# Two transformer layers on one core: which row maxima stand beside the projections, as sums of two key tiles, and in what order attention issues the rest

## The chip, the cores and the metric

The kernel runs on one core of a Trainium2 chip. The metric is the device time of one execution in microseconds (us). TensorE (PE) does the matrix products, VectorE (DVE) and ScalarE (ACT) read their results out of PSUM, GpSimd (POOL) works on SBUF alone, SyncE (SP) issues nearly all transfers. PSUM has eight banks; one bank holds one 128x512 result in fp32.

## The reference

Two rounds of attention and a squared-ReLU MLP, each behind a layer norm, with the same weights in both rounds:

```python
B, S, D, H = 1, 2048, 640, 32          # head width 20; F = 1536 in the MLP
qkv = layernorm(x) @ wqkv
scores = einsum("bhqd,bhkd->bhqk", q, k) * Dh ** -0.5
p = softmax(scores, axis=-1)
x = x + einsum("bhqk,bhkd->bhqd", p, v).reshape(B, S, D) @ wo
x = x + square(relu(layernorm(x) @ w1 + b1)) @ w2 + b2
```

## The kernel before

The kernel does the two layers one after the other. Each has three stages: projections (`qkv`), attention, and the output projection with the MLP. Most operands are split into a high and a low fp32r part, so that a projection is fifteen matmuls (five slices of D, three products each).

**Heads and blocks.** Four heads make a group `g` (8 of them), 512 queries a block of queries `qb` (4 of them). A block `t = 4 g + qb` is the unit of attention: 32 blocks, each with 16 key tiles of 128. Softmax needs the largest score of each query first. The scores for that are computed by queries: one matmul for 128 queries (`sub`, 4 of them), one head and 512 keys (`c`, 4 of them). Heads lie in two halves of the PE array (`par` 0 and 1), so that two matmuls run side by side, and a *pair* is both of them, for one `(p, sub)`. One block and one `c` are 8 pairs.

**Plain maxima and doubles.** A plain maximum is one matmul and one DVE reduction over 512 keys (line 679 beside the projections, `smax_two`; line 665 in attention, `smax`). A double takes two key tiles at once. `kd` holds the difference of key tiles 2i+1 and 2i; PE multiplies it with q (line 654), ACT takes the ReLU (`step_two`, line 687), PE multiplies tile 2i, and DVE adds both and takes the maximum (`both_two`, line 694). Since a + relu(b - a) = max(a, b), one DVE instruction, followed by a read of its accumulator on the same line, does the work of two reductions. "d" stands for tiles 0 and 1, "e" for 2 and 3. The differences are made on POOL when the projection of the second tile is read out of PSUM (`proj_end`, line 398 and the next two), stored to `d_kd` in DRAM and loaded again by heads (`load_kd`).

**The projection stage.** `UNITS` lists 40 units (10 slices of the outputs by 4 blocks of 512 tokens), the first four slices (`FIRST`) for each block of tokens first; sixteen steps for V follow. From unit 4 on each matmul is done as two halves of 64 rows that run side by side, the second half 22 steps behind the first (`Halves.LAG`). After each matmul `between(cost)` is called; when the sum of costs (1 for a unit's matmul, 0.65 for one of V) has used up the pace, `some()` puts one step of maxima into PE's queue: a plain pair (pace 4.2) or one half of a double, `step_two` or `both_two` (pace 1.97 each). `STEPS[n]` says after which unit which tiles are loaded and which lists of maxima begin. Before, 32 plain pairs begin after units 4, 5, 9 and 11, and 22 lists of doubles (176 pairs) after unit 12. Nothing waits in software: PE, DVE, ACT and SP each run their own queue in order.

**Attention.** The order of operations in attention is a string, `ORDER_OF_BLOCK`, repeated until the stage is done: `a` and `b` are one score matmul by keys of either half with its exponential on ACT (128x512), `S` is both with one exponential of 128x1024, `m` and `n` are one plain maximum of either half for a later block, and `V` is the product of weights and values for one key tile (eight matmuls, line 763, in column tiles of 32). I call the stretch from one `V` to the next a period; each has four scores on average. The banks are chosen by `Clock`, a small model of the queues in the kernel itself. `todo` lists the maxima that the projection stage has not done.

Of the kernel before, what the change touches and what calls it, by code (L numbers as in the profile page):

```python
# [9 lines left out]
F32R = mybir.dt.float32r  # L10
# [29 lines left out]
def tile_layers(  # L40
# [185 lines left out]
            sp.put(raw, k * 4, k * 4 + 2, 2, eng_hi, eng_lo)  # L226

    d_qk = dram.tile([2, 2, D, S], F32R, name="d_qk")
    d_kd = dram.tile([2, 2, 2 * P, QB], F32R, name="d_kd")
    d_v = dram.tile([S, H, 32], F32, name="d_v")  # L230
    d_o = dram.tile([D, NQB, 2 * QB], F32R, name="d_o")
    d_one = dram.tile([2, 2, QB], F32R, name="d_one")
# [150 lines left out]
    def proj_end(pos, tb, dst):  # L383
        ev = slot([P, 2, QB], F32R, "ev")
        which, jj = divmod(ORDER[pos], 5)
        rows = slice(jj * P, (jj + 1) * P)
        kd = None
        if which and pos < FIRST:


            if tb % 2 == 0 and jj == 0:
                keys["of"] = slot([P, 2, QB], F32, "kf")
            kf = keys["of"][:, jj, :]
            r = xtile("r")[:, :QB] if tb % 2 else kf
            split_on_pool(ev[:, 0, :], ev[:, 1, :], dst, r, nc.scalar.copy)
            if tb % 2:
                kd = slot([P, 2, QB], F32R, "kd")
                nc.gpsimd.tensor_sub(kf, r, kf)
                pool_hi(kd[:, 0, :], kf)
                pool_lo(kd[:, 1, :], kf, kd[:, 0, :].bitcast(F32))  # L400
                if jj:
                    del keys["of"]
        else:
            if tb or pos >= FIRST:
                split_on_pool(
                    ev[:, 0, :], ev[:, 1, :], dst, None, nc.scalar.copy if pos < FIRST else None
                )
# [423 lines left out]
    def prep_job():  # L831
# [13 lines left out]


    DOUBLE = [
        [],
# [5 lines left out]
    ]  # L854
    PARTLY = {g * NQB + qb for x in DOUBLE for g, qb, c in x}

    FIRST = 4
    PLAIN_PACE = 4.2  # L860
    DOUBLE_PACE = 1.97
    STEPS = {
        2: [("tiles", (0, 0, 0))],
        4: [("plain", (0, 0, 0)), ("tiles", (1, 0, 0))],
        5: [("plain", (1, 0, 0))],
        7: [("tiles", (0, 0, 1))],
        9: [("plain", (0, 0, 1)), ("tiles", (1, 0, 1))],
        10: [("tiles", (0, 1, "d"))],
        11: [("plain", (1, 0, 1))],
        12: [("double", 1)],  # L870
        15: [("double", 2)],
        19: [("double", 3)],
    }
    UNITS = [(tb, pos) for tb in range(NQB) for pos in range(FIRST)]
    UNITS += [(tb, pos) for pos in range(FIRST, 10) for tb in range(NQB)]

    def qkv(first, x_src, rest):

        pending, groups, work = [], [], []
        double, twos, begun = [], [], []  # L880
        left.update((t, 4) for t in range(NBLK))
        done.clear()
# [50 lines left out]
        def end_group(x):  # L933
            g, qb, c = x
            t = g * NQB + qb
            rest = [w[0] for w in work[:1] + twos[:1]] + [w[0][0] for w in begun[:1]] + groups + double
            if t == 0:
                left[t] -= 1 if c in range(4) else 2
                if left[t] == 0:
                    mrows_max(t)  # L940
                    store = mrows(t)
                    later_rows.append((state["n"] + 60, store))
                    later_rows.append((state["n"] + 75, lambda: mrows_load(t)))
            if (t or left[t]) and all(y[:2] != (g, qb) for y in rest[:4]):
                del q_t[t]
            use = {(y[0], y[2]) for y in rest + coming}
            use |= {(h, 2 * "de".index(y)) for h, y in use if y not in range(4)}
            for y in [y for y in k_t if y[0] == g and y not in use]:
                if g < 2 or y[1] not in range(4):
                    del k_t[y]  # L950
# [10 lines left out]
                queue.extend((x, p, sub) for p, sub in PAIRS)  # L961
            return queue.pop(0)

        def one():
            w = following(groups, work)
            if w:
                (g, qb, c), p, sub = w
                smax_two(g * NQB + qb, p, sub, c)
                done.add((g * NQB + qb, p, sub, c))
                if (p, sub) == PAIRS[-1]:  # L970
                    end_group(w[0])

        def some():


            while later_rows and later_rows[0][0] <= state["n"]:
                later_rows.pop(0)[1]()
            if begun and (len(begun) > 1 or not (double or twos)):
                w, r = begun.pop(0)
                (g, qb, x), p, sub = w  # L980
                t = g * NQB + qb
                both_two(t, p, sub, x, r)
                c = 2 * "de".index(x)
                done.update([(t, p, sub, c), (t, p, sub, c + 1)])
                if (p, sub) == PAIRS[-1]:
                    end_group(w[0])
                return DOUBLE_PACE
            if groups or work:
                one()
                return PLAIN_PACE  # L990
# [17 lines left out]
        for n, (tb, pos) in enumerate(UNITS):  # L1008
# [11 lines left out]
            for what, x in STEPS.get(n, ()):  # L1020
                if what == "tiles":
                    tiles(x)
                elif what == "plain":
                    groups.append(x)
# [6 lines left out]
        for tt in range(NKT):  # L1031
# [15 lines left out]
            if tt == 11:  # L1047
                load_k(3, 0, True)
                load_q(3 * NQB)
            if tt == 12:  # L1050
                for c in range(1, 4):
                    load_k(3, c, True)
            if tt == 13:
                load_q(1)
                load_q(3 * NQB + 1)
        while run.behind:
            run.catch()
        while double or twos or begun:
# [11 lines left out]


    ORDER_OF_BLOCK = (
        "bbannaVbamnabmVnabmnabVSnanbmVnambabmVSbmnaVSnabmVSnSmVbmamnSVbmanbanVan"
        "abmbmVbambannVbmabanmVSmbanVSnabmVSnSmVm"
    )

    def attention(first, x_src, first_rows):
        last = NBLK * NKT
# [117 lines left out]
        for o in "abab":  # L1196
            op(o)
        while state["done"] < last:
            for o in ORDER_OF_BLOCK:
                op(o)  # L1200
        assert min(sm_n) == len(todo)
        q_t.clear()
# [227 lines left out]
```

## Time and profile before

| what | value |
|---|---|
| median of 3 runs | 3586.14 us (3582.98 to 3586.66) |
| profiled execution, its own time | 3588.35 us |
| span of its trace | 3586.5 us |
| mean granted clock of TensorE | 0.998 |
| busy: PE, DVE, ACT, POOL | 99%, 74%, 75%, 23% |
| projection stage, first and second layer | to 341.7 us; 1805.9 to 2122.3 us |
| attention, first and second layer | 341.7 to 1386.0 us; 2122.3 to 3168.2 us |

The span runs from the first to the last instruction; 1.85 us of the profiled execution lie outside it. The ends of the stages are the first and the last exponential (line 758) and the first matmul of the second layer's projections. A busy PE is not PE at its peak, since ends of matmuls are modelled: what PE does is read from the distance between starts.

### The profile page before, as it was taken

How to read it: one execution, taken by the hardware profiler on the slowest of the kernel's cores; microseconds unless marked ns; L12 is line 12 of the kernel's file. 1: busy time of each engine (PE TensorE's matmuls, PEld its weight loads, DVE VectorE, ACT ScalarE, POOL GpSimd, SP SyncE). 2: the span in 40 equal slices, each digit the busy share in tenths (PEclk: the TensorE clock that was granted, in tenths of full speed). 3: DMA queues.
4: the chain of work that ended last, by engine and by line, in shares of the span. 5: the costliest groups of instructions: out<-in, count | busy, mean ns of one | idle time of the engine just before them, and what ended most of it. 6: DMA issues, size and time to landing. Idle time of an engine off the chain costs nothing.

```text
span 3586.5 us, 71057 instructions
## 1 busy us (share of the span) xinstructions
PE 3557.8 (99%) x25544; PEld 2151.0 (60%) x25544; DVE 2650.9 (74%) x5208; ACT 2694.0 (75%) x4742; POOL 836.0 (23%) x945
## 2 busy tenths in 40 slices
PE   8999999999999999999999999999999999999999
PEld 7998333333333336889989973333333333378998
DVE  8998888888888871445569988888888888625443
ACT  3888999999999994122238889999999999932221
POOL 5440334312121210122143201212112212101110
PEclk9999999999999999999999999999999999999999
DMA  7766454422212136622367552222222121365220
GB/s 242 231 223 198 138 170 147 141 78 71 60 49 60 54 102 218 234 74 74 103 193 226 191 174 67 79 73 63 67 83 56 42 60 51 111 234 209 75 81 37
DMA packets 282800, 433.85 MB, mean 121 GB/s; under 512 B 71188, under 2 KB 130324, under 8 KB 282448
## 3 DMA queue, kind: packets, MB, share of 16 engines
q1 hardware_dynamic: 281920, 427.61, 38.3%
q8 instruction: 202, 3.31, 0.4%
q10 hardware_dynamic: 528, 1.70, 0.2%
q14 instruction: 150, 1.23, 0.1%
HBM read 284.48 MB, written 144.68 MB: 120 GB/s over the span
## 4 chain that ended last, share of the span: by engine, by line
PE 94%; DMA 2%; DVE 1%; ACT 1%; SPq 0%; issue 0%; POOL 0%; ACTq 0%; DVEq 0%; POOLq 0%
PE banks L763 27%; PE banks L336 22%; PE banks L748 18%; PE banks L654 17%; PE banks L365 5%; PE banks L356 4%; ACT e L758 0%; SPq L76 0%; DMA k<-d_qk 0%; PE banks L461 0%; DMA ot<-d_o 0%; DVE r L1278 0%; DVE h L257 0%; ACT r L1277 0%; DVE mx L679 0%
## 5 line engine op out<-in xcount | busy, mean ns | idle before, releaser
L758 ACT ACTIVATE e<-banks 128x512 f32<-128x512 f32 (+1 forms) x3460 | 2040.8, 687 | 49.4 <-PE banks L748 11.5
L665 DVE TENSOR_REDUCE mx<-banks 128x1 f32<-128x512 f32 x2560 | 1620.7, 685 | 326.1 <-PE banks L654 294.4
L763 PE MATMUL banks<-e,vg 128*32 128x512 f32 x8192 | 1097.3, 605 | 6.1 <-ACT e L758 5.4
L654 PE MATMUL banks<-k,q 60*128 60x512 f32 x3392 | 1080.6, 411 | 6.3 <-DMA q<-d_qk 1.8
L748 PE MATMUL banks<-q,k 62*128 62x512 f32 x4096 | 1045.5, 441 | 0.0
L748 PEld LDWEIGHTS banks<-q,k 62*128 62x128 f32 x4096 | 514.5, 185 | 741.8 <-ACT e L758 467.6
L654 PEld LDWEIGHTS banks<-k,q 60*128 60x128 f32 x3392 | 579.3, 185 | 208.0 <-ACT e L758 64.7
L694 DVE CUSTOM_DVE_ANT_0 rl<-banks,rl 128x512 f32<-128x512 f32 x704 | 456.7, 688 | 24.5 <-PE banks L654 6.2
L687 ACT ACTIVATE rl<-banks 128x512 f32<-128x512 f32 x704 | 381.0, 601 | 52.3 <-PE banks L654 41.8
L763 PEld LDWEIGHTS banks<-e,vg 128*32 128x32 f32 x8192 | 163.8, 108 | 362.3 <-issue 262.6
L336 PE MATMUL banks<-w,h 128*128 128x320 f32 x2304 | 348.9, 310 | 2.6 <-DVE h L257 2.5
L1277 ACT ACTIVATE r<-banks,b_t 128x512 f32<-128x512 f32 x96 | 66.1, 688 | 377.8 <-PE banks L336 224.7
L336 PEld LDWEIGHTS banks<-w,h 128*128 128x128 f32 x2304 | 339.2, 188 | 11.4 <-DVE h L257 6.4
L336 PE MATMUL banks<-xnT,w 128*128 128x512 f32 x1440 | 329.7, 389 | 0.0
L365 PE MATMUL banks<-xnT,wqk 64*128 64x512 f32 x1080 | 327.3, 393 | 1.6 <-DVE turned_t L358 1.6
L356 PE MATMUL banks<-xnT,wqk 64*128 64x512 f32 x1080 | 327.2, 394 | 0.0
L336 PEld LDWEIGHTS banks<-xnT,w 128*128 128x128 f32 x1440 | 269.5, 188 | 55.3
L807 POOL TENSOR_TENSOR few<-few,minus_t 128x16 f32<-128x16 f32 x62 | 179.8, 2900 | 225.6 <-DMA few<-d_s 225.6
L654 PE MATMUL banks<-kd,q 60*128 60x512 f32 x704 | 208.9, 398 | 0.2
L365 PEld LDWEIGHTS banks<-xnT,wqk 64*128 64x128 f32 x1080 | 201.2, 187 | 12.9 <-DVE turned_t L358 2.1
L268 POOL CAST mr<-nt 128x32 fp32r<-128x32 f32 x64 | 13.4, 210 | 824.6 <-DVE nt L720 794.6
L356 PEld LDWEIGHTS banks<-xnT,wqk 64*128 64x128 f32 x1080 | 198.8, 186 | 10.2 <-issue 1.7
(91 smaller groups left out, 2789.5 us busy)
## 6 DMA issues: line engine op xcount, KB each, us to landing
q<-d_qk SPq DMA_DIRECT2D x888, 80.0 KB
d_qk<-ev SPq DMA_DIRECT2D x80, 512.0 KB
k<-d_qk SPq DMA_DIRECT2D x456, 80.0 KB
x<-d_x SPq DMA_DIRECT2D x96, 320.0 KB
d_o<-ot SPq DMA_DIRECT2D x248, 80.0 KB
ot<-d_o SPq DMA_DIRECT2D x38, 512.0 KB
d_v<-v SPq DMA_DIRECT2D x32, 512.0 KB
vg<-d_v SPq DMA_DIRECT2D x32, 512.0 KB
```

Source lines behind the costliest of these rows:

```text
L336: nc.tensor.matmul(dst, a, b, start=(n == 0), stop=(n == last))
L356: nc.tensor.matmul(dst, a[:64], b[:64], start=start, stop=last)
L365: nc.tensor.matmul(dst, a, b, start=False, stop=last, skip_group_check=True)
L654: nc.tensor.matmul(dst, q_t[t][b : b + 60, p, sub * P : (sub + 1) * P], k_t[t // NQB, c][b : b + 60, p, :], start=True, stop=True,)
L665: nc.vector.tensor_reduce(maxima(t)[:, 2 * p + par, sub, c : c + 1], dst, axis=AX.X, op=ALU.max)
L687: nc.scalar.activation(r, dst, AF.Relu)
L694: nc.vector.tensor_tensor_reduce(out=r[par], in0=dst, in1=r[par], scale=1.0, scalar=LEAST, op0=ALU.add, op1=ALU.max, accum_out=maxima(t)[: ...
L748: nc.tensor.matmul(dst, k_t[t // NQB, kt // 4][b : b + 62, p, (kt % 4) * P : (kt % 4 + 1) * P], q_t[t][b : b + 62, p, :], start=True, stop ...
L758: nc.scalar.activation(dst, src, AF.Exp, scale=SCALE)
L763: nc.tensor.matmul(acc[32 * h : 32 * h + 32, :], v_t[t // NQB, kt // 8][:, kt % 8, 32 * h : 32 * h + 32], es[p][:, par, :], start=(kt == 0 ...
L807: nc.gpsimd.tensor_tensor(few, few, minus_t, op=ALU.pow)
L1277: nc.scalar.activation(r, dst, AF.Relu, bias=b1_t[:, f : f + 1])
```

## The change

The plain maxima beside the projections go. In their place all of groups 0 to 2 are done by doubles, and the first block of group 3 too: 26 lists, 208 pairs. Differences are therefore made for a third slice of K as well (`jj` 2, which is unit 16 to 19), and `d_kd` grows by a third. The first list begins after unit 8, the pace of a double's half goes from 1.97 to 1.86. Attention has 1216 maxima per layer to do and not 1280; `ORDER_OF_BLOCK` has 20 pairs in 16 periods and not 21, and in another order, and once all maxima are done `LAST_ORDER` takes over, in which all scores go by `S`.

```diff
-    d_kd = dram.tile([2, 2, 2 * P, QB], F32R, name="d_kd")
+    d_kd = dram.tile([2, 2, 3 * P, QB], F32R, name="d_kd")
...
-        if which and pos < FIRST:
+        if which and jj < 3:
-            if tb % 2 == 0 and jj == 0:
+            if tb % 2 == 0 and jj != 1:
                 keys["of"] = slot([P, 2, QB], F32, "kf")
-            kf = keys["of"][:, jj, :]
+            kf = keys["of"][:, jj % 2, :]
             r = xtile("r")[:, :QB] if tb % 2 else kf
-            split_on_pool(ev[:, 0, :], ev[:, 1, :], dst, r, nc.scalar.copy)
+            split_on_pool(
+                ev[:, 0, :], ev[:, 1, :], dst, r, nc.scalar.copy if pos < FIRST else None
+            )
...
     DOUBLE = [
-        [],
-        [(0, 1, "d"), (1, 1, "d"), (2, 0, "d"), (2, 1, "d")],
+        [(0, 0, "d"), (0, 1, "d")],
+        [(1, 0, "d"), (1, 1, "d"), (2, 0, "d"), (2, 1, "d")],
         [(0, 2, "d"), (1, 2, "d"), (2, 2, "d")],
...
+        [(3, 0, "d"), (3, 0, "e")],
     ]
+    NEXT = [t for t in range(3 * NQB, NBLK) if (3, t - 3 * NQB, "e") not in DOUBLE[4]]
...
-    PLAIN_PACE = 4.2
-    DOUBLE_PACE = 1.97
+    DOUBLE_PACE = 1.86
     STEPS = {
-        2: [("tiles", (0, 0, 0))],
-        4: [("plain", (0, 0, 0)), ("tiles", (1, 0, 0))],
-        5: [("plain", (1, 0, 0))],
-        7: [("tiles", (0, 0, 1))],
-        9: [("plain", (0, 0, 1)), ("tiles", (1, 0, 1))],
-        10: [("tiles", (0, 1, "d"))],
-        11: [("plain", (1, 0, 1))],
+        7: [("tiles", (0, 0, "d"))],
+        8: [("double", 0)],
+        10: [("tiles", (1, 0, "d"))],
         12: [("double", 1)],
         15: [("double", 2)],
         19: [("double", 3)],
+        26: [("double", 4)],
     }
...
     ORDER_OF_BLOCK = (
-        "bbannaVbamnabmVnabmnabVSnanbmVnambabmVSbmnaVSnabmVSnSmVbmamnSVbmanbanVan"
-        "abmbmVbambannVbmabanmVSmbanVSnabmVSnSmVm"
+        "SnabmVSanmbVSanmbVSSmnVnabbanmVnabanmbVbabmnnaVnaabmbmVbmmbanaVnambmbaVb"
+        "amnmbaVnanbabmVSmnabVSmnabVSnabmVSanmbV"
     )
+    LAST_ORDER = "SSSVSSVSSVSV"
...
-            for o in ORDER_OF_BLOCK:
+            for o in LAST_ORDER if min(sm_n) == len(todo) else ORDER_OF_BLOCK:
                 op(o)
```

The loads of group 3's keys and queries at the end of the stage, and `end_group` and `some`, lose or gain what follows from that.

**PE, second layer, the first maxima beside the projections.** `xnT` are the transposed rows, `wqk` the weights, line 356 the first and line 365 the second half of a projection matmul. Before, early in unit 5:

```order
L356 MATMUL banks<-xnT_19059,wqk_18909 128x512 x2
L654 MATMUL banks<-k_19418,q_19425 128x512 x2
L356 MATMUL banks<-xnT_19059,wqk_18909 128x512
L356 MATMUL banks<-xnT_19062,wqk_18909 128x512 x2
L356 MATMUL banks<-xnT_19062,wqk_18918 128x512
```

Now, at the beginning of unit 9 (the maxima's matmul is line 656 in the changed kernel):

```order
L365 MATMUL banks<-xnT_19135,wqk_19027 128x512
L656 MATMUL banks<-kd_19675,q_19689 128x512 x2
L356 MATMUL banks<-xnT_19320,wqk_18979 128x512
L365 MATMUL banks<-xnT_19146,wqk_19027 128x512
L356 MATMUL banks<-xnT_19320,wqk_18979 128x512
L365 MATMUL banks<-xnT_19146,wqk_19027 128x512
L656 MATMUL banks<-kd_19675,q_19689 128x512 x2
```

The first maxima stand four units later, and the first operand that PE waits for is a difference tile, not a key tile.

**SP, second layer, the loads ahead of these.** `ev` is a projection on its way to DRAM (`d_qk`), `k`, `q` and `kd` are loads by heads, six transfers each. Before:

```order
L76 DMA d_qk<-ev_19381 128x2x512
L76 DMA k_19418<-d_qk 20x2x512 x6
L76 DMA q_19425<-d_qk 20x2x512 x6
L76 DMA d_qk<-ev_19414 128x2x512
L76 DMA d_qk<-ev_19449 128x2x512
L76 DMA k_19471<-d_qk 20x2x512 x6
L76 DMA q_19478<-d_qk 20x2x512 x6
```

Now:

```order
L76 DMA d_qk<-ev_19593 128x2x512
L76 DMA d_kd<-kd_19598 128x2x512
L76 DMA kd_19675<-d_kd 20x2x512 x6
L76 DMA k_19682<-d_qk 20x2x512 x6
L76 DMA q_19689<-d_qk 20x2x512 x6
L76 DMA d_qk<-ev_19651 128x2x512
```

The load of the difference stands right behind its own store, and the load of q behind that of the difference and of k; the two loads of plain key tiles and their queries that stood further ahead are gone.

More of the change, by code (lines that the diff above doesn't have):

```diff
@@ L877, in qkv @@
     def qkv(first, x_src, rest):
-        pending, groups, work = [], [], []
+        pending = []
         double, twos, begun = [], [], []
@@ L935, in end_group @@
             t = g * NQB + qb
-            rest = [w[0] for w in work[:1] + twos[:1]] + [w[0][0] for w in begun[:1]] + groups + double
+            rest = [w[0] for w in twos[:1]] + [w[0][0] for w in begun[:1]] + double
             if t == 0:
@@ L962, in following @@
             return queue.pop(0)
[L964 to L971, printed above, removed]
         def some():
@@ L987, in some @@
                 return DOUBLE_PACE
-            if groups or work:
-                one()
-                return PLAIN_PACE
             w = following(double, twos)
@@ L1022, in qkv @@
                     tiles(x)
-                elif what == "plain":
-                    groups.append(x)
                 else:
@@ L1046, in qkv @@
                     load_k(0, c, True)
[L1047 to L1052, printed above, removed]
+            if tt in (11, 12):
+                for c in (0, 1) if tt == 11 else (2, 3):
+                    if (3, c) not in k_t:
+                        load_k(3, c, True)
+                if tt == 11:
+                    load_q(NEXT[0])
             if tt == 13:
                 load_q(1)
-                load_q(3 * NQB + 1)
+                load_q(NEXT[1])
         while run.behind:
```

## The prediction

> **What bounds the kernel now.** I read the page first, then the engines' busy times by stage, then the order of time inside each stage. From the page, the chain that ended last:
>
> ```profile
> PE 94%; DMA 2%; DVE 1%; ACT 1%; SPq 0%; issue 0%; POOL 0%; ACTq 0%; DVEq 0%; POOLq 0%
> ```
>
> The chain stays on PE, but a busy PE says little here, so I look at what runs beside it. Busy times by stage (stretch, its length, then PE, PEld, DVE, ACT, POOL busy with instructions, the granted clock, DMA): the second layer's units with doubles, its V steps, its attention, and the first layer's attention.
>
> ```profile
> 1872.60:2007.60 135.00, 134.97 (x1143) 124.90 (x1141) 126.55 (x415) 116.84 (x223) 52.15 (x55) 1.00 0.70 227
> 2007.60:2122.30 114.70, 114.17 (x1305) 112.51 (x1302) 107.18 (x359) 96.15 (x193) 11.93 (x22) 0.99 0.59 190
> 2122.30:3168.20 1045.90, 1042.93 (x7414) 398.58 (x7412) 839.13 (x1373) 1020.33 (x1731) 202.14 (x186) 1.00 0.26 73
> 341.70:1386.00 1044.30, 1041.33 (x7413) 397.27 (x7411) 839.22 (x1373) 1020.42 (x1731) 273.44 (x290) 1.00 0.35 101
> ```
>
> Beside the projections DVE is 93 to 94% busy; in attention ACT is 97.7% busy (1020.42 of 1044.30) and DVE 80%. So two engines stand close to their limit in each stage. Which one waits in attention is seen in PE's order of time:
>
> ```profile
> 716.16 1.07 PE L763 MATMUL banks<-e,vg 128*32 128x512 f32 x8
> 717.15 0.72 PE L748 MATMUL banks<-q,k 62*128 62x512 f32 x3
> 717.50 0.61 PE L654 MATMUL banks<-k,q 60*128 60x512 f32 x2
> 717.73 0.40 PE L748 MATMUL banks<-q,k 62*128 62x512 f32 x1
> 718.06 1.07 PE L763 MATMUL banks<-e,vg 128*32 128x512 f32 x8
> ...
> 720.20 1.06 PE L763 MATMUL banks<-e,vg 128*32 128x512 f32 x8
> ```
>
> From V to V, a period with four scores and two maxima takes 1.90 us (three matmuls deep in each half of the array), the next, with four and three (four deep in one half), 2.14 us. A step of depth costs 0.24 us, and a seventh matmul costs as much as an eighth would. Per layer PE's order has 304 periods with seven matmuls, 182 with six and 26 others. At 1.90 for these too that makes 304 x 2.14 + 182 x 1.90 + 26 x 1.90 = 1045.8 us, against 1044.3 measured: attention is paced by PE's periods, with ACT just behind.
>
> Beside the projections the instructions of line 694 (two per maximum, so four per pair of doubles) tell the rate, first in the units, then in V's steps:
>
> ```profile
> 1872.60:2007.60 135.00, 124.24 (x381) 1.00 0.70 227
> 2016.02:2110.35 94.33, 90.89 (x279) 1.00 0.59 182
> ```
>
> That is 135.00 x 4 / 381 = 1.417 us per pair in the units and 94.33 x 4 / 279 = 1.352 in V's steps, where DVE is 96% busy with them. I take 1.352 as DVE's floor.
>
> **The change, part by part.** The sum is made against the profiled execution's own 3588.35 us, 0.06% over the median of 3586.14; I take the difference off at the end.
>
> *Attention.* Counted in PE's new order, a layer has 242 periods with seven matmuls, 243 with six and 27 others: 62 x 2.14 less, 61 x 1.90 and one of 1.90 more, so -14.9 us per layer, -30 in all. The last periods go by `S` alone; what they take now is this row:
>
> ```profile
> 1356.00:1384.00 28.00, 26.20 (x177) 7.42 (x174) 0.69 (x1) 28.00 (x52) 6.07 (x4) 1.00 0.58 178
> ```
>
> ACT is busy all the time there, and with 12 matmuls a period, 177 / 12 periods in 28.00 us are 1.90 us each. What `S` alone changes there no row prices; two exponentials in one instruction save an instruction's fixed part or nothing, over 14 periods at most 2 us per layer, and I take nothing. The ends: if ACT follows, up to -17 per layer; if it cannot in the new run of eight six-matmul periods (at most three stood in a row before), half is lost, -7.
>
> *Beside the projections, the rate.* 16 V steps hold 83 pairs now, the units 125, which makes 208. At pace 1.97 a pair stood on 3.94 projection matmuls; a whole one costs 0.229 us by this row (60 of them, no maxima beside):
>
> ```profile
> 1805.86:1819.58 13.72, 13.72 (x60) 11.08 (x60) 1.00 0.70 229
> ```
>
> 3.94 x 0.229 plus four maxima matmuls, two deep, 2 x 0.24, is 1.38; measured 1.417, 2.6% more. At pace 1.86, 3.72 x 0.229 + 0.48 = 1.33, with the same 2.6% 1.366, which is now next to DVE's floor of 1.352. I take 1.375 in the units (between 1.352 and the old 1.417) and 1.352 in V's steps: 125 x 1.375 + 83 x 1.352 = 284.1 us. The stage before, from the first ReLU of a double to the first exponential, is read from ACT's order of time:
>
> ```profile
> 92.50 2.05 ACT L687 ACTIVATE rl<-banks 128x512 f32<-128x512 f32 x4
> 341.75 4.52 ACT L758 ACTIVATE e<-banks 128x512 f32<-128x512 f32 x9
> 1872.60 3.03 ACT L687 ACTIVATE rl<-banks 128x512 f32<-128x512 f32 x6
> 2122.26 4.03 ACT L758 ACTIVATE e<-banks 128x512 f32<-128x512 f32 x8
> ```
>
> 249.3 and 249.7 us for 176 pairs, of which 97 at 1.417 and 79 at 1.352 are 244.3, and some 5 for the way in and out. Now 284.1 + 5 = 289.1, about 40 us longer in each layer. What can pay for that is an earlier start alone.
>
> *The start.* Before, plain maxima filled units 5 to 13. They are gone, and doubles begin in unit 9 as soon as PE has the first difference tile. In the second layer PE comes free early: units 4 to 8 are 75 matmuls, 17.2 us from 1819.58, plus 20 transposes,
>
> ```profile
> 1825.34 0.46 PE L654 MATMUL banks<-k,q 60*128 60x512 f32 x1 [1.03 <-DMA d_qk<-ev]
> 1830.88 1.53 PE L461 MATMUL banks<-ident,x 128*128 128x128 f32 x12
> ```
>
> 12 in 1.53, so some 2.6 us: unit 9 begins at about 1839. The difference comes late, since on POOL it stands behind three tiles that come from these transposes:
>
> ```profile
> 53.74 1.29 POOL L271 TENSOR_TENSOR kd<-kf,kd 128x512 fp32r<-128x512 f32 x1
> 1832.89 3.79 POOL L271 TENSOR_TENSOR xnT<-r,xnT 128x512 fp32r<-128x512 f32 x3 [13.99 <-PE banks L365]
> 1839.95 1.29 POOL L271 TENSOR_TENSOR kd<-kf,kd 128x512 fp32r<-128x512 f32 x1
> ```
>
> It was ready at 1841.2. Without the maxima ahead of the transposes (ten matmuls at 0.12) and the 1.5 us lost at the first of them (1823.84 to 1825.34, rows here and below) PE gets there 2.7 us earlier, say 3: 1838.2. In the first layer 55.0, less some 2.5, is 52.5. Then comes SP's queue, in the order that the change shows: store, load of the difference, of k, of q. What such steps take:
>
> ```profile
> 1812.12 2.47 SPq L76 DMA_DIRECT2D d_qk<-ev  x2
> 1814.88 2.65 SPq L76 DMA_DIRECT2D k<-d_qk  x6
> 1817.57 3.53 SPq L76 DMA_DIRECT2D q<-d_qk  x6
> 1821.57 0.89 SPq L76 DMA_DIRECT2D d_qk<-ev  x2
> 1826.44 2.19 SPq L76 DMA_DIRECT2D k<-d_qk  x6
> 1828.68 2.35 SPq L76 DMA_DIRECT2D q<-d_qk  x6
> 1823.84 0.47 PE L654 MATMUL banks<-k,q 60*128 60x512 f32 x1
> ```
>
> A load waits for the store that it reads: 4.9 us from 1821.57 to 1826.44, with two stores; I take 3.5 for one, between that and the 2.8 from 1812.12 to 1814.88. Twelve transfers take 2.19 + 2.35, 4.5 us with the gap. From the first transfer of q to PE's first matmul with it, 1817.57 to 1823.84, 6.3 us. Sum 14.3: the first double stands at about 1852.5 in the second layer and 66.8 in the first, its ReLU half a microsecond later. PE waits some 13 us at the top of unit 9, and behind that matmul in its queue stand unit 9's own matmuls, the lagging halves and, in the first layer, the third set of transposes; ACT and DVE have little else to do. So the doubles start 1872.6 - 1853.0 = 19.6 and 92.5 - 67.3 = 25.2 us earlier, and the stage gets 40 - 19.6 = 20.4 and 40 - 25.2 = 14.8 us longer. In the first layer ten copies of those transposes on ACT, each like the ReLU of the next row some 0.6 us, now lie among the first doubles; with half of that hidden, +3.
>
> ```profile
> L687 ACT ACTIVATE rl<-banks 128x512 f32<-128x512 f32 x704 | 381.0, 601 | 52.3 <-PE banks L654 41.8 <-PE banks L365 7.3 <-PE banks L356 0.6
> ```
>
> The wait has a second price. Where PE has little to do its granted clock falls, as at the way into the second attention (0.50 in the last but two columns, 28 matmuls in 6.8 us):
>
> ```profile
> 2120.60:2127.40 6.80, 6.80 (x28) 4.14 (x28) 1.63 (x4) 4.44 (x10) 0.47 (x2) 0.50 0.36 123
> ```
>
> I take 1 us per layer for the first doubles at such a clock (0 to 3.4, half of that stretch). [...]
>
> *What costs nothing.* The third slice's differences (two sets of four POOL instructions per layer, 0.6 to 1.3 us each as the rows of `kd` show) lie in a stretch where POOL is busy 52.15 of 135.00 us; without that cover they would cost 9 us. Two more stores and twelve more loads of differences on SP lie in units 17 to 30, where a load runs two lists ahead of its use; were one late, it would cost a wait like the one in unit 9.
>
> *Sum.* 20.4 + 14.8 + 3 + 2 - 30 = +10: 3588.35 + 10 = 3598.6, and 2.2 less for the median: 3596 us. About 0.2% (7 us) is what a measurement of this kernel can tell from no change.
>
> **The rivals.** *The doubles begin in time* (faster). If the difference, its load and q are there when PE reaches unit 9, at 1839 and about 52, both first ReLUs come some 13 us earlier still and the clock stays up: 3596 - 26 - 2 = 3568. For it: POOL waited 13.99 us ahead of the three tiles, so its chain may move further forward than I say, and fewer loads stand ahead in SP's queue. Against it: a store, eighteen transfers and a landing need over 10 us by the rows above, and the program leaves PE only three units, some 10 us, between the difference's projection and its use. It decides from the point where both first ReLUs come at or before 62 and 1848.
>
> *A draw.* The start is as I say but 3 us earlier in each layer, and the pace lifts the units to DVE's floor: 125 x (1.375 - 1.352) = 2.9 us per layer. 3596 - 6 - 5.8 = 3584, no change to be seen. For it: DVE ran at the floor for over 90 us in V's steps. Against it: ACT has 116.84 of 135.00 us to do at the old pace, and the first units lay it another copy and cast per unit between the ReLUs.
>
> *ACT takes attention over* (slower still). To shorten attention by 15 us ACT must be busy 1020 of 1029 us, and in eight periods in a row it gets 1.90 us for four exponentials, what the last periods show as its own rate. Then half of the gain goes: 3596 + 15 = 3611. Against it: single runs of three such periods held 1.90, and in the eight longer periods that follow ACT can catch up.
>
> **How the numbers follow.** My forecast, 3596, has 0.43; the doubles in time 0.18; the draw 0.24; ACT's limit 0.15. Faster by over 0.2% is the first rival, 0.18; within 0.2% the draw, 0.24; slower the forecast and the last, 0.58. The range leaves out the first rival: below it goes to the draw with attention at its -17 per layer and a start 2 us earlier yet (3584 - 4 - 4 = 3576), above to ACT's limit with 1.40 us per pair in the units (3611 + 2 x 3 = 3617, cut to 3614).
>
> **What would show it.** Right: first ReLUs of the doubles near 67 and 1853 with PE waiting over 10 us for a transfer of `kd` or q and the clock at one half behind it; the first exponentials 18 and 20 us later than before; 1.35 to 1.40 us per pair; the attention stages near 1029 us, with 1.90 for periods of six. Wrong: PE without a wait in unit 9; pairs over 1.42; attention over 1036 us, or six-matmul periods over 1.95.

## The result, and the profile after

The changed kernel takes 3608.68 us (median of 4 runs, 3607.94 to 3610.58) against 3586.05 us before: ratio 1.0066, 95% interval 1.0048 to 1.0083. It is slower by 0.66%. The forecast was 3596, within 3576 to 3614. The span of the changed kernel's trace is 3608.1 us; the traced execution took 3610.58 us, 1.9 over the median.

The chain that ended last, from the page of the changed kernel, still stays on PE:

```profile
PE 93%; ACT 2%; DMA 2%; POOL 1%; DVE 1%; issue 1%; SPq 1%; ACTq 0%; POOLq 0%; DVEq 0%
```

Where the time came from is read as before, from the first ReLU of a double and the first exponential of each layer in ACT's order of time (start, length, engine, line, operation; the bracket is idle time and what ended it):

```profile
64.36 0.60 ACT L689 ACTIVATE rl<-banks 128x512 f32<-128x512 f32 x1 [11.79 <-PE banks L656]
369.08 3.48 ACT L760 ACTIVATE e<-banks 128x512 f32<-128x512 f32 x6
1865.11 0.60 ACT L689 ACTIVATE rl<-banks 128x512 f32<-128x512 f32 x1 [11.81 <-PE banks L656]
2159.46 3.97 ACT L760 ACTIVATE e<-banks 128x512 f32<-128x512 f32 x7
```

The first layer's first exponential is 27.3 us later (341.75 before). The second layer's projections begin at 1819.79, so that its stage takes 339.7 us, 23.3 more than the 316.4 before. Attention, by engine in the stretch between these (length, then PE, PEld, DVE, ACT, POOL busy, the granted clock, DMA):

```profile
369.10:1398.90 1029.80, 1027.89 (x7348) 384.15 (x7347) 802.15 (x1309) 1011.10 (x1740) 273.93 (x290) 1.00 0.34 101
2159.50:3189.00 1029.50, 1027.64 (x7348) 384.17 (x7347) 801.91 (x1309) 1010.76 (x1739) 202.61 (x186) 1.00 0.26 73
```

From the first to the last exponential (start to start) it was 1043.5 and 1045.2 us and is 1029.8 and 1029.6: 13.8 and 15.6 less. So 27.3 + 23.3 - 13.8 - 15.6 = 21.2 of the 21.6 us by which the span grew; the MLP is as it was. Its periods are what was forecast; PE's order of time in two periods of six matmuls in a row:

```profile
717.43 1.07 PE L765 MATMUL banks<-e,vg 128*32 128x512 f32 x8
718.42 0.50 PE L750 MATMUL banks<-q,k 62*128 62x512 f32 x2
718.76 0.40 PE L656 MATMUL banks<-k,q 60*128 60x512 f32 x2
719.00 0.39 PE L750 MATMUL banks<-q,k 62*128 62x512 f32 x2
719.32 1.06 PE L765 MATMUL banks<-e,vg 128*32 128x512 f32 x8
...
721.20 1.06 PE L765 MATMUL banks<-e,vg 128*32 128x512 f32 x8
```

From V to V 1.89 and 1.88 us. At the top of unit 9, PE's waits between 30 and 95 us and between 1815 and 1885 us (waiting instruction, what it waits for: us in total, times, longest):

```profile
PE banks L656 <- DMA q<-d_qk: 10.7, 2, 10.2
PE banks L656 <- DMA q<-d_qk: 11.0, 2, 10.2
```

In the second layer PE's first double starts at 1864.25 us. SP's order of time ahead of it (start of the issue, length):

```profile
1852.28 0.36 SPq L76 DMA_DIRECT2D d_kd<-kd  x1
1855.11 2.19 SPq L76 DMA_DIRECT2D kd<-d_kd  x6
1857.34 2.23 SPq L76 DMA_DIRECT2D k<-d_qk  x6
1859.67 2.50 SPq L76 DMA_DIRECT2D q<-d_qk  x6
```

And the clock around the second layer's wait, in three stretches (the number before the last two is the granted clock):

```profile
1858.10:1865.10 7.00, 0.76 (x1) 0.28 (x1) 0.00 (x0) 0.00 (x0) 2.17 (x3) 0.50 0.67 208
1865.10:1871.80 6.70, 6.08 (x28) 5.20 (x30) 1.86 (x5) 4.12 (x8) 0.55 (x1) 0.50 0.57 180
1871.80:1875.00 3.20, 3.20 (x30) 3.13 (x28) 2.99 (x12) 2.69 (x6) 0.74 (x1) 1.00 0.88 336
```

It stays at one half for 6.7 us behind the wait. The instructions of DVE's line 696 (four per pair) give the rate in three stretches of the second layer: units 10 to 17, units 18 to 38, V's steps.

```profile
1873.50:1922.00 48.50, 41.84 (x130) 1.00 0.71 234
1922.00:2037.00 115.00, 108.58 (x337) 1.00 0.62 196
2051.50:2148.60 97.10, 94.42 (x295) 1.00 0.59 171
```

That is 48.50 x 4 / 130 = 1.49 us per pair, then 1.365, then 1.317. Later the rate is a little better than forecast; in the first eight units it is much worse. Units 18 to 38 of the kernel before, by its line 694:

```profile
1890.90:2002.30 111.40, 103.86 (x321) 1.00 0.72 233
```

That is 111.40 x 4 / 321 = 1.388 us per pair, so that the change gained little there. The 1.417 of the prediction is a mean with slower units, ahead of these and behind them.

### The profile page after: what moved, and what is told of

The parts are those of the page before. It is cut to its first block, busy times and chain, and to the rows that moved or that the text cites. A ratio compares the mean times of both kernels' runs of the same rounds, so it can differ in the third digit from the quotient of the medians.

```text
span 3608.1 us, 71289 instructions
## 1 busy us (share of the span) xinstructions
PE 3558.6 (99%) x25544; PEld 2141.9 (59%) x25544; DVE 2577.4 (71%) x5210; ACT 2743.2 (76%) x4888; POOL 849.7 (24%) x957
## 4 chain that ended last, share of the span: by engine, by line
PE 93%; ACT 2%; DMA 2%; POOL 1%; DVE 1%; issue 1%; SPq 1%; ACTq 0%; POOLq 0%; DVEq 0%
PE banks L765 27%; PE banks L336 21%; PE banks L750 18%; PE banks L656 16%; PE banks L365 5%; PE banks L356 4%; ACT e L760 1%; PE banks L351 1%; SPq L76 1%; PE banks L463 0%; DMA k<-d_qk 0%; DVE h L257 0%; DVE r L1265 0%; ACT r L1264 0%; ACT rl L689 0%
## 5 line engine op out<-in xcount | busy, mean ns | idle before, releaser
L667 DVE TENSOR_REDUCE mx<-banks 128x1 f32<-128x512 f32 x2432 | 1547.5, 685 | 371.5 <-PE banks L656 290.3
L656 PE MATMUL banks<-k,q 60*128 60x512 f32 x3264 | 947.6, 409 | 0.2
L656 PEld LDWEIGHTS banks<-k,q 60*128 60x128 f32 x3264 | 511.9, 185 | 293.4 <-ACT e L760 201.7
L696 DVE CUSTOM_DVE_ANT_0 rl<-banks,rl 128x512 f32<-128x512 f32 x832 | 534.5, 687 | 63.1 <-PE banks L656 44.1
L689 ACT ACTIVATE rl<-banks 128x512 f32<-128x512 f32 x832 | 449.7, 601 | 85.9 <-PE banks L656 73.2
L336 PEld LDWEIGHTS banks<-w,h 128*128 128x128 f32 x2304 | 339.2, 188 | 11.4 <-DVE h L257 6.4
L356 PE MATMUL banks<-xnT,wqk 64*128 64x512 f32 x1080 | 340.6, 400 | 1.3 <-ACT r L263 1.3
L365 PE MATMUL banks<-xnT,wqk 64*128 64x512 f32 x1080 | 339.3, 397 | 0.0
L336 PEld LDWEIGHTS banks<-xnT,w 128*128 128x128 f32 x1440 | 269.6, 188 | 55.3
L656 PE MATMUL banks<-kd,q 60*128 60x512 f32 x832 | 240.8, 411 | 28.2 <-DMA q<-d_qk 21.7
L365 PEld LDWEIGHTS banks<-xnT,wqk 64*128 64x128 f32 x1080 | 204.0, 189 | 11.6 <-DVE turned_t L358 0.4
L820 POOL TENSOR_TENSOR o<-o 128x512 f32<-128x512 f32 x62 | 79.6, 1284 | 517.6 <-DMA o<-d_r 283.1
```

Of the source, the lines that this page charges most:

```text
L336: nc.tensor.matmul(dst, a, b, start=(n == 0), stop=(n == last))
L356: nc.tensor.matmul(dst, a[:64], b[:64], start=start, stop=last)
L365: nc.tensor.matmul(dst, a, b, start=False, stop=last, skip_group_check=True)
L656: nc.tensor.matmul(dst, q_t[t][b : b + 60, p, sub * P : (sub + 1) * P], k_t[t // NQB, c][b : b + 60, p, :], start=True, stop=True,)
L667: nc.vector.tensor_reduce(maxima(t)[:, 2 * p + par, sub, c : c + 1], dst, axis=AX.X, op=ALU.max)
L689: nc.scalar.activation(r, dst, AF.Relu)
```

## The experiments

All kernels below have the changed kernel's 1216 maxima per layer in attention. Two readings of the projection stage were to be told apart. Theory 1 is the prediction's: from the first double on, the engines that read PSUM set a rate per pair, and only the first ReLU's time counts. Theory 2: PE's own matmuls set the end, so that each microsecond in which PE waits is lost. The table has the medians, the time of the traced execution (which lies up to 7 us from the median), and from its trace, read as above, the first ReLU and the first exponential (first layer: from the span's start; second: from the first matmul of its projections), and attention from the first to the last exponential.

| kernel | median us | traced us | ReLU, 1st | exp, 1st | ReLU, 2nd | exp, 2nd | attention |
|---|---|---|---|---|---|---|---|
| before | 3586.05 | 3588.35 | 92.5 | 341.8 | 66.7 | 316.4 | 1043.5, 1045.2 |
| changed | 3608.68 | 3610.58 | 64.4 | 369.1 | 45.3 | 339.7 | 1029.8, 1029.6 |
| old order of attention | 3631.77 | 3631.55 | 65.3 | 367.3 | 45.2 | 339.3 | 1040.4, 1040.6 |
| no order for the last periods | 3610.97 | 3610.22 | 65.0 | 367.0 | 45.4 | 339.3 | 1031.4, 1031.1 |
| later start, second list late | 3604.40 | 3611.34 | 69.7 | 365.5 | 45.4 | 340.8 | 1030.0, 1033.3 |
| later start, mended | 3593.53 | 3592.70 | 69.8 | 357.9 | 45.4 | 333.4 | 1030.2, 1029.5 |
| casts on POOL | 3600.13 | 3600.76 | 65.0 | 363.1 | 45.6 | 335.9 | 1030.0, 1029.7 |
| later start and casts | 3585.82 | 3586.21 | 70.1 | 354.1 | 44.8 | 330.5 | 1030.1, 1029.4 |
| 32 plain, 192 doubles | 3588.48 | 3594.95 | 92.4 | 356.1 | 64.9 | 328.5 | 1032.4, 1032.8 |
| the same and casts | 3584.93 | 3587.28 | 91.5 | 353.2 | 64.9 | 326.9 | 1031.4, 1032.1 |
| 16 plain, 200 doubles | 3593.77 | 3593.76 | 80.6 | 358.9 | 55.3 | 332.1 | 1030.6, 1029.6 |
| the same and casts | 3587.10 | 3585.94 | 79.9 | 355.3 | 55.5 | 329.2 | 1030.0, 1029.6 |
| 85 identity matmuls in the wait | 3622.51 | 3624.13 | 72.9 | 375.5 | 53.9 | 345.3 | 1029.9, 1029.5 |
| 42 identity matmuls in the wait | 3609.70 | 3610.30 | 65.4 | 369.3 | 46.0 | 339.2 | 1029.5, 1029.5 |

Two cautions go with the table. The kernel before was run again beside each group of kernels, with medians of 3585.56 to 3587.21 us, so that a difference of less than 2 us between two rows' medians tells nothing. And the changed kernel and the two below it have the same projections: from the first ReLU to the first exponential their traces take 304.7, 302.0 and 302.0 us in the first layer and 294.4, 294.1 and 293.9 in the second. So much can two executions differ.

**The old order of attention.** The order as before, with the changed kernel's projections.

```diff
-        "SnabmVSanmbVSanmbVSSmnVnabbanmVnabanmbVbabmnnaVnaabmbmVbmmbanaVnambmbaVb"
-        "amnmbaVnanbabmVSmnabVSmnabVSnabmVSanmbV"
+        "bbannaVbamnabmVnabmnabVSnanbmVnambabmVSbmnaVSnabmVSnSmVbmamnSVbmanbanVan"
+        "abmbmVbambannVbmabanmVSmbanVSnabmVSnSmVm"
...
-    LAST_ORDER = "SSSVSSVSSVSV"
```

> The changed kernel with the old order of attention (21 pairs in 16 periods) and no order for the last periods; the projections stay as changed. Theory (PE's periods pace attention): per layer 289 periods of seven matmuls, 173 of six and 50 others instead of 242, 243 and 27, so 47 x 0.24 = 11.3 us longer per layer, attention near 1042, the whole near 3608.7 + 23 = 3631. Rival (the gain comes from the 64 maxima less per layer, whatever the order): attention stays within 3 us of 1031, the whole 3609 to 3615.

3631.77 us, ratio to before 1.0127 (1.0112 to 1.0142); attention 10.6 and 11.0 us longer than in the changed kernel. Fewer maxima alone bring 3.2 and 4.6 us of the 13.8 and 15.6, since the old order still has 289 periods of seven matmuls: it is the periods that price attention, as the expectation had it (3631). The same stretch as above, with ACT busy 1017.52 of 1040.30 us:

```profile
367.30:1407.60 1040.30, 1034.32 (x7349) 390.14 (x7347) 798.72 (x1309) 1017.52 (x1730) 273.76 (x290) 1.00 0.35 102
```

**No order for the last periods.**

```diff
-            for o in LAST_ORDER if min(sm_n) == len(todo) else ORDER_OF_BLOCK:
+            for o in ORDER_OF_BLOCK:
```

> The changed kernel without the order for the last periods: they go in the new order, with its single exponentials, once all maxima are done. The prediction had bounded this at 0 to 2 us per layer and taken nothing: 3608.7 to 3612.7. By the changed kernel's last block, 29.6 us against 31.0 before, it is 1.4 us per layer: 3611.5.

3610.97 us, ratio 1.0066 (1.0052 to 1.008); attention 1.6 and 1.5 us longer per layer. `S` alone is worth that much, where the prediction had taken nothing; in the kernel before an exponential of 128x512 takes 608 ns on average and one of 128x1024 1036 ns. This rests on the stretches of attention: the ratios of the whole kernels, 1.0066 both, do not part the two.

**A later start.**

```diff
-        8: [("double", 0)],
-        10: [("tiles", (1, 0, "d"))],
+        10: [("double", 0), ("tiles", (1, 0, "d"))],
...
-    DOUBLE_PACE = 1.86
+    DOUBLE_PACE = 1.79
```

> The changed kernel with the first list of doubles begun after unit 10, not 8, and pace 1.79 instead of 1.86, so that PE does units 9 and 10 while the difference tile and q are on their way. Theory 1 (from the first double on the evicting engines' rate per pair sets the end): the first ReLU stands at the same 64 and 1865 us, 208 pairs follow at the same rate, and only the half clock is saved, about 3 us per layer: near 3602. Theory 2 (PE's wait at unit 9 is itself what the stage loses): two units of 3.4 us move into the wait, with the clock 10 us per layer: near 3588.

3604.4 us, ratio 1.0049 (1.0032 to 1.0066). It looks like theory 1, but it decides nothing: SP's queue has the next group's tiles ahead of the second list's query tile, and PE waited for that one too, some 4 us in unit 12. SP's order of time, and PE's waits from 1855 to 1892 us, those for the first list among them (the traced execution took 7 us more than the median):

```profile
1866.66 2.19 SPq L76 DMA_DIRECT2D kd<-d_kd  x6
1868.89 2.23 SPq L76 DMA_DIRECT2D k<-d_qk  x6
1871.50 5.46 SPq L76 DMA_DIRECT2D q<-d_qk  x12
```

```profile
PE banks L656 <- DMA q<-d_qk: 8.5, 4, 3.7
```

So it was made again with the loads in another order:

```diff
-        8: [("double", 0)],
-        10: [("tiles", (1, 0, "d"))],
+        8: [("tiles", (0, 1, "d"))],
+        10: [("double", 0)],
+        11: [("tiles", (1, 0, "d"))],
...
-    DOUBLE_PACE = 1.86
+    DOUBLE_PACE = 1.79
```

> As the kernel with the first list after unit 10 (pace 1.79), but the second list's query tile is loaded right behind the first's and ahead of the next group's tiles, since there its second list came late. Theory 1 (rate per pair from the first double on): the first ReLU stays at 64 to 70 and 45 us after the stages' starts, 208 x 1.36 + 5 = 288 us follow, plus 1 or 2 for ACT's extra work, so 3 to 5 us per layer less than in the changed kernel: 3598 to 3602. Theory 2 (PE's wait itself): 10 us per layer less, 3588.

3593.53 us, ratio 1.002 (1.0011 to 1.003): 15 us less than the changed kernel, between the two figures. PE's wait in the second layer, in the same window as above:

```profile
PE banks L656 <- DMA q<-d_qk: 3.7, 2, 3.3
```

Of 11.0 us 3.7 are left, and the stage is 6.3 us shorter, though the first ReLU stands where it stood. Theory 1 had that at 3 to 5. The first layer's stage is 11.2 us shorter; 3.7 of these are a stall, told below, that not every trace has. The edit moves the start, the loads and the pace together; no run has one of them alone. Units 18 to 38 and V's steps of this kernel, by DVE's line 696:

```profile
1899.00:2017.10 118.10, 112.75 (x355) 1.00 0.67 219
2031.60:2131.10 99.50, 97.56 (x305) 1.00 0.56 173
```

118.10 x 4 / 355 = 1.331 and 99.50 x 4 / 305 = 1.305 us per pair. With the denser order the pairs go faster, so the 1.352 that the prediction called DVE's floor was no floor. At 1.305 DVE's line is 98% busy (97.56 of 99.50 us); how much faster it could go no run shows. What PE does in the wait is therefore gained for the most part, and theory 2 is right in this. Its price of a pair, 0.48 us of PE's matmuls, is not borne out: units 18 to 38 take 111.4, 115.0 and 118.1 us with 80.25, 84.25 and 88.75 pairs in the kernel before, the changed one and this one, so that one more pair costs 0.7 to 0.9 us, between PE's 0.48 and theory 1's rate of 1.35. What makes up the rest, no run shows. Theory 2's 3 us for the clock could come in part at most: over the 17 us around the wait the clock is 0.80 on average, which, if it is 1.00 or 0.50 at any time, is an estimated 7 us at one half.

```profile
1849.00:1866.00 17.00, 13.10 (x85) 10.23 (x81) 7.35 (x26) 9.21 (x18) 4.56 (x4) 0.80 0.69 242
```

**Casts on POOL.** For the projections of blocks of tokens 2 and 3 (units 8 to 15) ACT only copies, and POOL casts:

```diff
-                ev[:, 0, :], ev[:, 1, :], dst, r, nc.scalar.copy if pos < FIRST else None
+                ev[:, 0, :], ev[:, 1, :], dst, r, nc.scalar.copy if pos < FIRST and tb < 2 else None
```

(and the same in the other call).

> The changed kernel with the cast to the high part of the projections of units 8 to 15 on POOL instead of ACT. Theory (ACT's copy and cast between the ReLUs make units 10 to 17 take 6.0 us and not 5.5): these units come down to about 5.5, 4.5 us less per layer, near 3600. Rival (these units are slow for another reason, the clock or PE's own work): no change, 3609; if POOL's longer chain makes difference tiles late, up to 5 us per layer slower, 3619.

3600.13 us, ratio 1.004 (1.0025 to 1.0055). ACT's casts (line 264) in units 10 to 17 of the changed kernel and of this one, then DVE's line 696 in the latter's units 10 to 17:

```profile
1873.50:1922.00 48.50, 4.96 (x8) 1.00 0.71 234
```

```profile
1867.80:1912.50 44.70, 0.00 (x0) 1.00 0.75 247
1867.80:1912.50 44.70, 41.65 (x129) 1.00 0.75 247
```

Eight casts gone, eight units shorter by 3.8 us: 44.70 x 4 / 129 = 1.386 us per pair, near the later units' rate. DVE's waits in these stretches say how it works, in the changed kernel and in this one:

```profile
DVE rl L696 <- PE banks L656: 3.8, 7, 1.0
```

```profile
DVE rl L696 <- PE banks L656: 1.0, 3, 0.6
```

A cast of 0.6 us stands in ACT's queue ahead of a ReLU, PE's next pair waits for that ReLU's bank, and DVE for the pair. PE's own waits for a ReLU there are 2.0 us in the changed kernel, five of them. The same units of the first layer go from 48.7 to 44.7 us. That the first layer's stage is 6.0 us shorter in all owes the rest to the changed kernel's trace: the two others with the same projections have 302.0 us from ReLU to exponential, and this one has 298.1, which is 3.9 less.

**Plain maxima kept.** The kernel before, with group 3's two lists, their differences and the changed kernel's attention: 32 plain pairs, 192 doubles. Against the kernel before:

```diff
+        [(3, 0, "d"), (3, 0, "e")],
...
-    DOUBLE_PACE = 1.97
+    DOUBLE_PACE = 1.81
...
+        26: [("double", 4)],
```

> The plain maxima of the kernel before stay beside the projections (32 pairs in units 5 to 13), doubles begin after unit 12 as before, with 192 pairs (group 3's two lists added) at pace 1.81; attention is the changed kernel's, with the same 1216 maxima. Theory 1 (rate per pair): first ReLUs of doubles at 92.5 and 66.7 us after the stages' starts as before, then 192 x 1.37 + 5 = 268 us, so the first exponentials 8.6 and 5 us earlier than in the changed kernel: near 3595. Theory 2 (PE's own time): 16 pairs of 0.48 us more than before per layer, 7.7 us, so first exponentials 19.7 and 15.6 us earlier than in the changed kernel: near 3573.

3588.48 us, ratio 1.0009 (1.0 to 1.0018), between the two figures again (3595 and 3573): 20 us less than the changed kernel. From the first ReLU to the first exponential it takes 263.6 us in both layers for 192 pairs; at theory 1's rate it would be 268. So with the plain maxima left where they were the same 64 maxima move out of attention at next to no loss. In its trace the stages are 14.3 and 12.1 us longer than before, where 16 pairs at 0.48 would be 7.7. Attention is there 2.6 and 3.2 us longer than in the changed kernel; at its beginning in the first layer the clock stands at one half for 10.1 us, in an execution 6.5 us over the median of the ten:

```profile
353.70:363.80 10.10, 9.88 (x40) 4.76 (x39) 3.01 (x6) 6.29 (x11) 0.46 (x2) 0.50 0.61 176
```

**Sixteen plain pairs.** Only block 0 of group 0 by plain maxima, doubles from unit 11 on. Against the kernel with 32 plain pairs:

```diff
-        [(0, 1, "d"), (1, 1, "d"), (2, 0, "d"), (2, 1, "d")],
+        [(0, 1, "d"), (1, 0, "d"), (1, 1, "d"), (2, 0, "d"), (2, 1, "d")],
...
-    DOUBLE_PACE = 1.81
+    DOUBLE_PACE = 1.85
...
-        4: [("plain", (0, 0, 0)), ("tiles", (1, 0, 0))],
-        5: [("plain", (1, 0, 0))],
+        4: [("plain", (0, 0, 0))],
         7: [("tiles", (0, 0, 1))],
-        9: [("plain", (0, 0, 1)), ("tiles", (1, 0, 1))],
-        10: [("tiles", (0, 1, "d"))],
-        11: [("plain", (1, 0, 1))],
-        12: [("double", 1)],
+        8: [("plain", (0, 0, 1)), ("tiles", (0, 1, "d"))],
+        10: [("double", 1)],
```

> Between the two: 16 plain pairs (the first block of group 0) in units 5 to 11, then 200 double pairs from unit 11 on at pace 1.85; attention as changed, with the same 1216 maxima. Theory 1 (rate per pair): first ReLUs near 76 and 47 us after the stages' starts, then 200 x 1.36 + 5 = 277 us: first exponentials near 353 and 324 us, against 356.1 and 328.5 with 32 plain pairs: near 3581, faster than both kernels. Theory 2 (PE's own time): 16 plain pairs of 0.24 us for 8 of 0.48 us, the same as with 32 plain pairs, near 3588. If the difference tile or q still comes late (first ReLU after 52 in the second layer): 3590 or more.

3593.77 us, ratio 1.002 (1.0011 to 1.003): the third case of the expectation. PE waits in unit 9 for the tiles of the second plain list, and the first ReLU comes at 55.3 us:

```profile
1852.46 0.76 PE L656 MATMUL banks<-k,q 60*128 60x512 f32 x1 [5.33 <-DMA q<-d_qk]
```

**Casts on POOL, with each of the three.**

> The kernel with 16 plain and 200 double pairs, with the casts of units 8 to 15 on POOL as well. If ACT's copies and casts slow the first units with doubles here too, 2 to 4 us less per layer than with 16 plain pairs alone: near 3575. If POOL's longer chain makes the difference tiles late: the same or up to 5 us slower.

> The changed kernel with both repairs: first list after unit 10 with the second list's query tile loaded early, and the casts of units 8 to 15 on POOL. Units 12 to 17 took 6.2 us with the first repair alone; at 1.36 us per pair they would take 5.7: 3 us less per layer, near 3587.5, level with the kernel before. If the two repairs give back the same loss: 3593, as with the first alone.

> 32 plain pairs and 192 double pairs as in the run with the plain maxima kept, with the casts of units 8 to 15 on POOL. There only units 14 to 18 lay ACT's extra work between the ReLUs (5.9 us and not 5.5): 2 us less per layer, near 3584.5, a little faster than both kernels. If ACT's work is hidden there: 3588.5.

These are 16 plain, later start and 32 plain, in this order. 3587.10 us, 3585.82 us and 3584.93 us, with ratios to before of 1.0004 (0.9995 to 1.0013), 0.9997 (0.9988 to 1.0006) and 0.9994 (0.9985 to 1.0003): 6.7, 7.7 and 3.6 us less than without. The two repairs of the changed kernel add up (15.2 and 8.6 us alone, 22.9 together). The 3575 expected of the first was missed, since it was reckoned from the 3581 that the kernel without the casts did not reach. The last is the best of all kernels run and beats the changed one, but its interval does not part it from the kernel before.

**Identity matmuls in the wait.**

```diff
                 (g, qb, x), p, sub = w
+                if (w == ((0, 0, "d"), 0, 0)):
+                    warm(85)
```

> The changed kernel with 85 matmuls of 128x128 on the identity (0.11 us each, 9.6 us) ahead of the first double in PE's queue, whose result nobody reads; they lie in the wait for the first operands, so that PE is not idle there. If the half clock costs time after the wait, 5.2 us of it in the first layer and 6.7 in the second lie behind the first maxima, and half of each comes back: 6 us in all, near 3603. By the prediction's 1 us per layer: 3607. If the evicting engines set the rate there anyway: no change, 3609.

3622.51 us, ratio 1.01 (1.0085 to 1.0116), and none of the three figures: the size was misjudged, since each identity matmul stands as two instructions in the trace, and the first ReLU came 8.6 us later. The clock was full behind it,

```profile
1879.00:1886.00 7.00, 6.68 (x53) 5.33 (x54) 3.55 (x11) 5.29 (x11) 1.28 (x1) 1.00 0.15 58
```

and from first ReLU to first exponential 2.1 and 3.0 us were gained. With `warm(42)`:

> As the kernel with matmuls on the identity in PE's wait, but half as many, since each of them stood as two instructions in the trace and 18 us were too long for the wait: 42 of them, 9.5 us. First ReLUs back at 64.4 and 45.3 us after the stages' starts. If the half clock behind the wait costs the 2.1 and 3.0 us that the longer version gave back between first ReLU and first exponential: near 3603.5. If that was only the later start at work: 3609.

3609.70 us, ratio 1.006 (1.0046 to 1.0073): no change, and 0.9 and 1.2 us less from first ReLU to first exponential. The clock behind the wait, however, was not full throughout:

```profile
1854.35 9.64 PE L480 MATMUL banks<-ident 128*128 128x128 f32 x84
1865.59 0.47 PE L656 MATMUL banks<-kd,q 60*128 60x512 f32 x1 [1.59 <-DMA q<-d_qk]
1866.70 0.47 PE L656 MATMUL banks<-kd,q 60*128 60x512 f32 x1 [0.64 <-DMA q<-d_qk]
```

```profile
1868.00:1871.50 3.50, 3.50 (x20) 3.14 (x18) 1.79 (x5) 2.61 (x6) 0.49 (x1) 0.52 0.48 143
```

The first layer's 2.1 and 0.9 us tell nothing, since the same projections differ by 2.7 us between traces. In the second layer, where they differ by 0.5, half of the stretch at half clock is gone for about 1 us, all of it for 2.5 to 3, of which some may come from loads that were further ahead. So the half clock costs an estimated 1 to 3 us per layer. The table has a second reading. In the first layer of the kernel with 32 plain pairs attention begins with 10.1 us at one half (the row there) and takes 1032.4 us; in the changed kernel, in whose two attention stages the clock is 1.00, it takes 1029.8 and 1029.6. The 2.6 and 2.8 us are about a quarter of that stretch, which for the 6.7 us behind the wait makes an estimated 2 us.

## Why the prediction was right, and where it was off

The forecast missed by 12.7 us inside its range. Point by point:

- **Attention, -14.9 per layer:** measured -13.8 and -15.6. The sum held, its parts less so. `LAST_ORDER`, taken as nothing, is worth 1.5 us of it; the periods alone brought 12.1 and 14.1. Against the run without it, the old order's 47 more periods of seven cost 9.0 and 9.5 us, 0.20 each where 0.24 was taken. ACT did not take attention over, though it is busy 1011 of 1030 us. That the second layer gained more fits the clock: before, its attention begins with 6.8 us at one half (the prediction's own row), the first layer's does not (1.00 from 341.7 to 374.5 us).
- **The start:** forecast 67.3 and 47.1 us (1853.0 on the old time axis) for the first ReLUs, measured 64.4 and 45.3; PE's wait forecast at some 13 us, measured 10.7 and 11.0, behind the store of the difference, its load, k and q in SP's queue. Neither the rival with the doubles in time nor the draw came.
- **From first ReLU to first exponential:** the mis-sized term. Forecast 289.1 plus 1 for the clock, and 3 for the first layer's transposes: 290 and 293. Measured 294.4 and 304.7, so 4.3 and 11.6 us more (302.0 and not 304.7 in the two other traces with the same projections, so about 9 in the first layer there). With the earlier starts (1.8 and 2.9) set against it, and 0.4 for attention, that is 11.6 of the 12.7 us.
- What was in it: the rates of the steady part came out better than taken (1.365 for 1.375, 1.317 for 1.352: over 84.25 and 73.75 pairs 3.4 us less). But units 10 to 17 went at 1.49 (over 32.5 pairs 3.8 us more), which is past the 1.42 that the prediction names as a sign of being wrong. That these two nearly cancel is luck. The slow units come of ACT's casts; the prediction named this extra copy and cast, but only as evidence against one rival, and gave it no price in its sum. The run with the casts on POOL shows 3.8 us of it in the second layer and 4.0 in the first.
- In the first layer two more things were missing. The third set of transposes lies in unit 9 with the first doubles: from the first ReLU to unit 10 it took 14.1 us against 8.4 in the second layer, 5.7 where 3 were taken. And at 243 us ACT's ReLU waited for POOL, which itself had waited for a store:

```profile
POOL wv L271 <- DMA d_qk<-ev: 6.3, 1, 6.3
...
ACT rl L689 <- POOL wv L271: 2.6, 1, 2.6
```

  Unit 39 and the first step of V take 18.2 us there against 14.5 in the second layer, and 14.5 in the first layer of the mended later start. That is 3.7 us from a queue that the prediction did not look at: the splitting of V's weights on ACT and POOL. It is not the same in every execution: with the same projections the stretch takes 15.2 us in the run without the order for the last periods and 15.8 with the old order.
- **The reason behind the number was wrong in one step:** "I take 1.352 as DVE's floor". DVE's line was 96% busy there, but with a denser order it went at 1.305. The forecast therefore let the rate of pairs set the length of the stage from the first double on, and PE's wait cost nothing in it but a later start. The runs show the wait as mostly lost time that another order can give back: with 7.3 of its 11.0 us filled the second layer's stage is 6.3 us shorter. By PE's matmuls alone the exchange would be a gain: 32 more double pairs at 0.48 less 32 plain ones at 0.24 are 7.7 us per layer against 14.9 in attention. Against the 7.2 us that this leaves stand, in the second layer, 11.0 in the wait, 3.8 for ACT's casts and 1 to 3 for the clock: with the 7.7 they make 23.5 to 25.5 us, and the stage is 23.3 longer than before. That is an estimate, since one more pair cost more than 0.48 where it could be read, and no kernel that was run got the gain.

## What to carry to other kernels

PE's wait of 11.0 us at the head of its queue was lost for the most part: with 7.3 us of it filled, the second layer's stage was 6.3 us shorter. Moving two units of ready work ahead of it, with the loads in the right order and a denser pace behind, gave back 15 of 23 us. DVE's busy share of 96% was no floor: with a denser supply its 1.352 us per pair became 1.305, so try that before you call a rate a floor. A mean over a stage can hide a slow part that the change makes longer, as the 1.417 did. When work moves to an earlier place, look at what the engine between (here ACT) already has to do there, and give it a price in the sum.

## What the runs showed of the hardware

The prediction let the granted clock fall where PE has little to do, and gave a row with the half clock in which PE is busy for all 6.80 us. In the changed kernel's first wait, from 55.80 to 69.60 us, PE was busy for 5.52 of 13.80 us and the clock was 0.51 on average. Two traces have the half clock after idle times of less than 2 us as well. In the run with 42 identity matmuls PE idled 1.59 and 0.64 us, and about 1.4 us after the second the clock stood at 0.52 for 3.5 us; in the changed kernel's first layer one idle time of 1.78 us, ahead of 245.70, was followed by this stretch:

```profile
245.70 0.50 PE L656 MATMUL banks<-kd,q 60*128 60x512 f32 x1 [1.78 <-ACT rl L689]
```

```profile
247.10:250.40 3.30, 3.30 (x20) 2.87 (x18) 2.26 (x8) 1.80 (x5) 1.89 (x2) 0.50 0.99 376
```

The run with 42 identity matmuls has the same stall, 1.81 us long, and its clock is 1.00 behind it, so that between these two traces the length of the idle time alone does not decide it:

```profile
247.14 0.50 PE L656 MATMUL banks<-kd,q 60*128 60x512 f32 x1 [1.81 <-ACT rl L689]
```

```profile
247.10:250.50 3.40, 3.36 (x28) 2.76 (x29) 2.23 (x7) 3.03 (x7) 2.13 (x3) 1.00 1.04 390
```
